# Four-token loads for nine units, shifts in a weight conversion, and low halves on GpSimd: a gated linear attention with FFN on one core

## The chip, the cores and the metric

The kernel runs on one core of a Trainium2 chip. The metric is the time of one execution on the device in microseconds (us). A core has five engines with instruction queues of their own: TensorE (PE, matmuls), VectorE (DVE), ScalarE (ACT), GpSimd (POOL) and SyncE (SP, which here issues the DMAs). Data lies in SBUF, matmul results in PSUM.

## The reference

Attention runs over batch, head and time with a decaying state of 48 x 48; its output, put together by token, goes through a feed-forward network (FFN).

```python
B, H, S, D = 4, 8, 768, 48
for t in range(S):
    state = alpha[:, :, t, :, None] * state + np.einsum('bhd,bhe->bhde', k[:, :, t], v[:, :, t])
    y[:, :, t] = np.einsum('bhd,bhde->bhe', q[:, :, t], state)
x = y.transpose(0, 2, 1, 3).reshape(B * S, H * D)     # 3072 x 384
h = x @ w_in                                          # w_in 384 x 2048, float64
g = np.maximum(0.01 * h, h)
out = (g @ w_out).astype(np.float32)                  # w_out 2048 x 384, float64
```

## The kernel before, in words

**Units and blocks.** A unit is 128 tokens of one batch entry, all 8 heads: 6 time blocks by 4 entries, 24 units. Three units make a block of 384 tokens for the FFN, 8 blocks in all. The hidden width of 2048 is cut into 16 pieces of 128, counted by f; (i, f) is the FFN item of block i and piece f.

**A unit** (`attention`) is written as steps that a generator yields. `scans` turns alpha so that the head dimension lies on partitions and time along the row, and makes the running products `pc` (L309) and the reverse sums `rc` (L315). `scaled_q` and `scaled_k` turn q and k and multiply them by `pc` and `rc`. `scores` and `mask_scores` make and mask the 128 x 128 scores (PE L351, ACT L361, POOL L362), `outputs` the result and its split into xh and xl (L419, L420), `next_state` the new state (`us` at L430 or L432, scaled on POOL at L367). Tiles of loads have two buffers each for alpha, q and k, three for v; the load of unit u+2 is asked for as soon as unit u's tile has been turned.

For the first nine units (`AHEAD`) a load puts a token's row in a partition: 128 x 8 runs of 48 numbers (192 bytes). `transposed` turns such a tile by four PE transposes of 128 x 128 (L272). For the later units four tokens follow one another in a run, and DVE turns them (L284, STREAM_TRANSPOSE).

**Weights.** They come as float64 words in the tile `raw` (four buffers), and `converting` makes of each piece f a high and a low part (`w`, 128 x 768 each): ACT scales the upper words in place (L238); DVE makes the float32 `bits` (L240, L243); ACT rounds these to the matmul format, `hi` (L246); DVE takes the exponent, `pw` (L250), subtracts `hi` from the value (L252), scales the lower words by `pw` (L254) and adds both into `lo` (L257). All DVE operations here are 128 x 768.

**An FFN item.** `ffn_in` runs nine matmuls of 384 columns into `ph` (L487): for each of three row groups high x xh, high x xl, low x xh. ACT makes `t` = 0.01 ph (L490), DVE the maximum (L493), ACT the high half `gh` (L495), DVE the low half `gl` = t - gh (L499). `ffn_out` runs nine matmuls of 384 columns (L512) three items later (`LAG`); `gl` has four buffers, `t` two.

**The order.** A scheduler sets the order on each engine from the program's order and its own estimates; `issue_after` holds an instruction behind another in it. First come nine units (the front); the weights of pieces 0 and 1 are loaded and converted among the last of them, and item (0,0) and (1,0) too. Then the items of blocks 0 and 1 alternate, (0, f), (1, f), while piece by piece is loaded and converted; `put` writes these DVE and ACT steps one behind another in a fixed line. From block 2 on attention of units 9 to 23 is cut in slices between items; its first eight steps are held behind the `gl` of the item before (`behind("gl", ...)`).

Of the kernel before, what the change touches and what calls it, by code (L numbers as in the profile page):

```python
# [22 lines left out]
def gated_linear_attn_ffn(ctx, tc, q, k, v, alpha, w_in, w_out, out):  # L23
# [31 lines left out]
    T4 = 4  # L55
# [1 line left out]
    PITCH = RUN + GAP  # L57
    AHEAD = 3 * UPB
    LAG = 3
    SOON, EARLY = 2, 2  # L60
    LEAD = 8
    SL = 8 * UPB

# [52 lines left out]
    def load(u, i):  # L116
        if u >= NU:
            return
        if u >= AHEAD and later is not None:
            later.append((load, u, i))  # L120
            return
        tb, b = units[u]
        ts = slice(tb * C, (tb + 1) * C)
        t, src = loaded(u, i), (alpha, q, k)[i]
        if u < AHEAD:
            n = H if u or i else H // 2
            for h in range(0, H, n):
                nc.sync.dma_start(
                    by_token(t)[:, h:h + n, 0:D], src[b, h:h + n, ts, :].rearrange("h t d -> t h d")
                )  # L130
            return

        for a in range(4):
            off = 32 * (a % 2)
            nc.sync.dma_start(
                t[32 * a:32 * (a + 1), :].rearrange("j (p r) -> j p r", p=NP)[:, :, 0:RUN - off],
                src[b, a // 2::2, ts, :].rearrange("p (j t) d -> j p (t d)", t=T4)[:, :, off:],
            )
# [12 lines left out]

    nc.vector.memset(seed, 0.0)
    nc.vector.memset(ones, 1.0)
    zeros = cst.tile([P, 4 * C], F32R, name="zeros")
    nc.gpsimd.memset(zeros.bitcast(F32), 0.0)

    idle = ps_h.tile([P, 512], F32, name="ph")

# [2 lines left out]
        for _ in range(n):  # L161
            nc.tensor.matmul(idle[:, 0:C], seed[:, 0, :], seed[:, 1, :], start=True, stop=True)

    def keep_warm_wide(n):

        for _ in range(2):
            nc.tensor.matmul(idle[:, 0:n], zeros[:, 0:P], zeros[:, 0:n], start=True, stop=True)

    keep_warm(6)
    for i in (0, 1, 2):  # L170
        for t in loads_sb[i]:
            nc.vector.memset(by_token(t)[:, :, D:], 1.0)
    for n in range(max(NL)):
        for i in range(3):
            if n < NL[i]:
# [7 lines left out]
    )  # L183
    for i in (0, 1, 2):
        for t in loads_sb[i]:
            nc.gpsimd.memset(t[:, H * HB:], 1.0)


    runs = [(0, D, 0, 1, D), (D, GAP, NG * D, NG, 1), (HB, D, NP * D, 1, D), (BR, GAP, (NP + NG) * D, NG, 1)]
# [29 lines left out]
    def converting(f, ordered=False):  # L219

        if f >= NF:
            return
        raw = jobs.pop(f)
        w_sb[f] = cst.tile([P, 2, 2 * DM], F32R, name=f"w{f}")
        hi, lo = w_sb[f][:, HIGH, :], w_sb[f][:, LOW, :]
        if not f64:
            val = raw[:, :, 0:P].bitcast(F32)
            hi, lo = (t.rearrange("p (g f) -> p g f", f=P) for t in (hi, lo))
            nc.scalar.copy(hi, val)
            made["w", f] = nc.vector.tensor_tensor(lo, val, hi.bitcast(F32), ALU.subtract)  # L230
            return
        words = raw.rearrange("p g (f w) -> p (g f) w", w=2)
        top, low = words[:, :, 1], words[:, :, 0]
        bits = cvp.tile([P, 2 * DM], I32, name="bits", bufs=NBITS)
        val = bits.bitcast(F32)

        with nullcontext() if lines["ACT"] else behind("hi", f - 1):
            put(ordered, "ACT", lambda: nc.scalar.mul(top.bitcast(F32), top.bitcast(F32), 2.0 ** -112))  # L238
        yield
        put(ordered, "DVE", lambda: nc.vector.tensor_scalar(  # L240
            bits, top, 3, 0x7FFFFFF8, ALU.logical_shift_left, ALU.bitwise_and))
        yield
        put(ordered, "DVE", lambda: nc.vector.scalar_tensor_tensor(  # L243
            bits, top, -0x80000000, bits, ALU.bitwise_and, ALU.bitwise_or))
        yield
        made["hi", f] = put(ordered, "ACT", lambda: nc.scalar.copy(hi, val))  # L246
        yield
        pw = cvp.tile([P, 2 * DM], I32, name="pw", bufs=NPW)
        rest = pw.bitcast(F32)
        put(ordered, "DVE", lambda: nc.vector.tensor_scalar(pw, bits, -0x800000, None, ALU.bitwise_and))  # L250
        yield
        put(ordered, "DVE", lambda: nc.vector.tensor_tensor(val, val, hi.bitcast(F32), ALU.subtract))  # L252
        yield
        put(ordered, "DVE", lambda: nc.vector.scalar_tensor_tensor(  # L254
            rest, low.bitcast(U32), 2.0 ** -52, rest, ALU.mult, ALU.mult))
        yield
        made["w", f] = put(ordered, "DVE", lambda: nc.vector.tensor_tensor(lo, rest, val, ALU.add))  # L257

    def convert(f):
        for _ in converting(f):  # L260
# [5 lines left out]
    def transposed(u, i, name, **kw):  # L266

        src = loaded(u, i)
        if u < AHEAD:
            ps = banks4()  # L270
            for p in range(NP):
                last = nc.tensor.transpose(  # L272
                    ps[:, p, :], by_token(src)[:, 2 * p:2 * p + 2, :].rearrange("t h d -> t (h d)"), ident
                )
                if u == 0 and p % 2:
                    with tc.issue_after(last.ins):
                        if i == 2:
                            keep_warm_wide(4 * C if p == 1 else 2 * C)
                        else:
                            keep_warm(2)  # L280
            return ps
        t = atp.tile([P, NP, C], F32, name=name, **kw)
        src = src.rearrange("r (p n) -> r p n", p=NP)[:, :, 0:RUN]
        nc.vector.transpose(  # L284
            t.rearrange("r p (j t) -> r p t j", t=T4),
            src.rearrange("r p (t d) -> r p t d", t=T4)[:, :, :, 0:32],
        )
        return t
# [189 lines left out]
    def ffn_in(i, f, steps=None):  # L478

        ordered = steps is not None  # L480
        first, second = steps or ((), ())
        xh, xl = xs[i]
        ph = ps_h.tile([P, 512], F32, name="ph")[:, 0:TB]
        n = 0
        for g in range(NG):
            for wn, xt in ((HIGH, xh), (HIGH, xl), (LOW, xh)):
                nc.tensor.matmul(ph, w_in_of(f, wn, g), xt[:, g, :], start=n == 0, stop=n == 3 * NG - 1)  # L487
                n += 1
        t = ffp.tile([P, TB], F32, name="t")
        put(ordered, "ACT", lambda: nc.scalar.mul(t, ph, 0.01))  # L490
        for step in first:
            next(step, None)
        put(ordered, "DVE", lambda: nc.vector.tensor_tensor(t, ph, t, ALU.max))  # L493
        gh = ffp.tile([P, TB], F32R, name="gh", bufs=LAG + 1)
        put(ordered, "ACT", lambda: nc.scalar.copy(gh, t))  # L495
        for step in second:
            next(step, None)
        gl = ffp.tile([P, TB], F32R, name="gl", bufs=LAG + 1)
        made["gl", i, f] = put(ordered, "DVE", lambda: nc.vector.tensor_tensor(gl, t, gh.bitcast(F32), ALU.subtract))  # L499
        return gh, gl  # L500

    pos = {}
# [53 lines left out]
                gs[len(gs)] = ffn_in(i, f)  # L556
    kinds[:] = "a"

    with behind("x", AHEAD - 1):
        for _ in converting(EARLY, True):  # L560
            pass

    due, emitted, held = 0.0, 0, 0
    new, coming = None, converting(EARLY + 1, True)
    next(coming)
    for n in range(len(items) + LAG):
        slices = 0
        if n < len(items):
            i, f, slices, _ = items[n]
            if f == 0:  # L570
                if i == 2:
                    st, held = attention(AHEAD, NU), 8
                while i not in ready:
                    next(st)
                emitted, due = 0, 0.0
            if loaded_f < NF:
                load_weights(loaded_f)
                loaded_f += 1
                if loaded_f == NF:
                    asked, later = later, None  # L580
                    with behind("raw", NF - 1):
                        for fn, *args in asked:
                            fn(*args)
            if n < len(STARTS):
                pass
            elif i == 0:
                old, new, coming = new or iter(()), coming, converting(f + SOON + 1, True)
                gs[n] = ffn_in(i, f, ((), (coming, new, old, new)))
            elif i == 1:
                gs[n] = ffn_in(i, f, ((new, new), (new,)))  # L590
                next(new, None)
            else:
                gs[n] = ffn_in(i, f)
        for half in range(2):
            due += slices / 2
            while emitted < due:

                with behind("gl", *items[n - 1][:2]) if held else nullcontext():
                    next(st, None)
                held = max(held - 1, 0)  # L600
                emitted += 1
            if half == 0 and n >= LAG:
                i, f, _, tag = items[n - LAG]
                ffn_out(i, f, gs.pop(n - LAG), tag)
# [131 lines left out]
```

## Time and profile before

| what | value |
|---|---|
| median of 3 runs | 540.11 us (539.74 to 540.44) |
| the profiled execution | 538.77 us |
| its span in the profile | 537.1 us |
| PE busy | 518.8 us (97%) |
| DVE busy | 375.0 us (70%) |
| ACT busy | 234.0 us (44%) |
| POOL busy | 49.1 us (9%) |
| DMA, mean over the span | 87 GB/s |

The profile shows one execution, whose span begins with its first and ends with its last instruction. PE is busy nearly all the time; what it does not fill lies mostly in the first 80 us, so a reader should go by stretches of the span, not by shares of the whole. A row of instructions gives line, engine, operation, the tile written and the tiles read, the busy time and the mean of one in ns, and the idle time of that engine ahead of it with what ended it. The chain is followed back from the last instruction: each piece has its start, its length and what it was.

### The profile page before, as it was taken

The page shows a single profiled execution, that of the slowest core. Times are in us where ns is not written, and L with a number is a line of the kernel's source. Part 1 is how long each engine was busy: PE and PEld are TensorE (multiplying, and loading weights), DVE is VectorE, ACT ScalarE, POOL GpSimd, SP SyncE. Part 2 cuts the span into 40 slices and gives each one's busy share as a digit, 9 for nine tenths or more (in the row PEclk, how much of TensorE's full clock was granted, in tenths as well). Part 3 has the DMA queues.
Part 4 walks back from the last instruction along what each step waited for, and adds up shares of the span by engine and source line. Part 5 has one row for each costly group of instructions (what it writes and reads, how often), then busy time and mean ns, then how long its engine had stood idle before and what let it go on. Part 6 is the DMA issues. An engine that isn't in the chain of part 4 may idle for free.

```text
span 537.1 us, 10383 instructions
## 1 busy us (share of the span) xinstructions
PE 518.8 (97%) x3934; PEld 492.6 (92%) x3934; DVE 375.0 (70%) x703; ACT 234.0 (44%) x514; POOL 49.1 (9%) x116
## 2 busy tenths in 40 slices
PE   8879899999999999999999999999999999999995
PEld 7668789999999899999999999999999999999995
DVE  6778999999988897875675685775777534332331
ACT  2665755555533453435334443344343354233331
POOL 3333510000000011010000001000000000000000
PEclk9999899999999999999999999999999999999998
DMA  9999854454823643533323422523201010001001
GB/s 149 163 179 183 198 140 119 117 131 136 183 53 87 190 117 78 107 81 98 70 67 70 108 69 64 98 50 92 71 0 38 11 35 1 22 1 45 1 1 49
DMA packets 92985, 46.67 MB, mean 87 GB/s; under 512 B 57856, under 2 KB 90112, under 8 KB 92928
## 3 DMA queue, kind: packets, MB, share of 16 engines
q1 hardware_dynamic: 92928, 45.93, 39.0%
q8 instruction: 33, 0.54, 0.4%
q14 instruction: 24, 0.20, 0.1%
HBM read 38.83 MB, written 4.72 MB: 81 GB/s over the span
## 4 chain that ended last, share of the span: by engine, by line
PE 86%; DVE 4%; DMA 3%; issue 2%; ACT 1%; SPq 1%; POOL 1%; ACTq 0%; DVEq 0%; POOLq 0%
PE ph L487 36%; PE b L512 32%; PE a L390 5%; PE a L351 4%; PE a L512 4%; DMA small<-in_alpha_dram 2%; DMA raw<-in_moe_w_in_dram 1%; PE a L374 1%; PE b L272 1%; PE a L411 1%; PE b L390 1%; DVE pc L309 1%; PE b L411 1%; POOL sm L362 1%; DVE rc L315 0%
## 5 line engine op out<-in xcount | busy, mean ns | idle before, releaser
L487 PE MATMUL ph<-large,w 128*128 128x384 f32 x1152 | 227.4, 340 | 2.8 <-DVE t L493 2.8
L487 PEld LDWEIGHTS ph<-large,w 128*128 128x128 f32 x1152 | 201.9, 189 | 5.5 <-DVE t L493 3.9
L512 PE MATMUL b<-w,gh 128*128 128x384 f32 x672 | 170.0, 340 | 0.0
L493 DVE TENSOR_TENSOR t<-ph,t 128x384 f32<-128x384 f32 x128 | 70.5, 551 | 88.7 <-ACT t L490 88.4
L512 PEld LDWEIGHTS b<-w,gh 128*128 128x128 f32 x672 | 119.7, 188 | 2.2 <-issue 0.5
L490 ACT ACTIVATE t<-ph 128x384 f32<-128x384 f32 x128 | 62.6, 489 | 130.1 <-PE ph L487 122.8
L495 ACT CAST gh<-t 128x384 fp32r<-128x384 f32 x128 | 65.7, 514 | 112.8 <-DVE t L493 102.6
L512 PE MATMUL b<-w,gl 128*128 128x384 f32 x336 | 107.4, 336 | 0.0
L499 DVE TENSOR_TENSOR gl<-t,gh 128x384 fp32r<-128x384 f32 x128 | 70.8, 553 | 34.4 <-ACT gh L495 33.2
L512 PEld LDWEIGHTS b<-w,gl 128*128 128x128 f32 x336 | 62.5, 188 | 0.1
L362 POOL TENSOR_SCALAR_AFFINE_SELECT sm<-sm 128x512 f32<-128x512 f32 x33 | 22.8, 705 | 113.3 <-ACT sm L361 113.3
L351 PE MATMUL a<-qs,ks 48*128 48x128 f32 x312 | 30.9, 287 | 0.1
L351 PEld LDWEIGHTS a<-qs,ks 48*128 48x128 f32 x312 | 25.9, 189 | 5.4 <-issue 4.4
L284 DVE STREAM_TRANSPOSE ks<-small 128x512 f32<-128x512 f32 x15 | 16.6, 1121 | 12.3 <-PE a L374 12.3
L390 PE MATMUL a<-sm,small 128*48 128x128 f32 (+1 forms) x312 | 23.2, 282 | 0.1
L319 POOL COPY pe<-pc 128x4 f32<-128x4 f32 x24 | 4.8, 202 | 188.6 <-DVE pc L309 188.6
L309 DVE TENSOR_TENSOR_SCAN pc<-e,small 128x128 f32<-128x128 f32 x60 | 20.1, 398 | 0.5 <-ACT pc L327 0.5
L367 POOL TENSOR_TENSOR small<-us,pe 112x192 f32<-112x192 f32 x20 | 11.9, 594 | 90.2 <-DVE us L432 87.5
L390 PEld LDWEIGHTS a<-sm,small 128*48 128x48 f32 (+1 forms) x312 | 17.1, 132 | 3.2 <-issue 3.0
L361 ACT COPY sm<-a 128x512 f32<-128x512 f32 x24 | 14.0, 585 | 13.8 <-PE b L351 11.1
L512 PE MATMUL a<-w,gh 128*128 128x384 f32 x96 | 20.0, 336 | 0.0
L315 DVE TENSOR_TENSOR_SCAN rc<-e,small 128x511 f32<-128x511 f32 x15 | 19.0, 1270 | 0.2
(86 smaller groups left out, 525.4 us busy)
## 6 DMA issues: line engine op xcount, KB each, us to landing
raw<-in_moe_w_out_dram SPq DMA_DIRECT2D x16, 384.0 KB, 3.9
small<-in_v_dram SPq DMA_DIRECT2D x24, 192.0 KB, 4.0
raw<-in_moe_w_in_dram SPq DMA_DIRECT2D x32, 144.0 KB, 3.9
out_dram<-t SPq DMA_DIRECT2D x24, 192.0 KB, 1.9
small<-in_alpha_dram SPq DMA_DIRECT2D x32, 96.0 KB, 2.3
small<-in_q_dram SPq DMA_DIRECT2D x30, 96.0 KB, 2.2
small<-in_k_dram SPq DMA_DIRECT2D x30, 96.0 KB, 2.2
small<-in_alpha_dram SPq DMA_DIRECT2D x30, 80.0 KB, 2.3
```

What stands on the lines that cost most here:

```text
L284: nc.vector.transpose(t.rearrange("r p (j t) -> r p t j", t=T4), src.rearrange("r p (t d) -> r p t d", t=T4)[:, :, :, 0:32],)
L309: nc.vector.tensor_tensor_scan(pc[:, p, :], aT[:, p, :], ones.broadcast_to([P, C]), 1.0, ALU.mult, ALU.mult)
L315: nc.vector.tensor_tensor_scan(flat[2][:, NP * C - 2::-1], flat[0][:, NP * C - 1:0:-1], flat[1][:, NP * C - 2::-1], last, ALU.mult, ALU.add)
L351: nc.tensor.matmul(ss[s][:, p, :], ks[lo:lo + D, p, :], qs[lo:lo + D, p, :], start=True, stop=True)
L362: nc.gpsimd.affine_select(out=sm[s], in_=sm[s], compare_op=ALU.is_ge, fill=0.0, base=0, pattern=[[0, NP], [1, C]], channel_multiplier=-1)
L390: nc.tensor.matmul(y[s][HB * c:HB * c + lhsT.shape[-1], p % 2, :], lhsT, rhs, skip_group_check=True, **kw)
L487: nc.tensor.matmul(ph, w_in_of(f, wn, g), xt[:, g, :], start=n == 0, stop=n == 3 * NG - 1)
L490: put(ordered, "ACT", lambda: nc.scalar.mul(t, ph, 0.01))
L493: put(ordered, "DVE", lambda: nc.vector.tensor_tensor(t, ph, t, ALU.max))
L495: put(ordered, "ACT", lambda: nc.scalar.copy(gh, t))
L499: made["gl", i, f] = put(ordered, "DVE", lambda: nc.vector.tensor_tensor(gl, t, gh.bitcast(F32), ALU.subtract))
L512: nc.tensor.matmul(po[j], gt[:, js], w_out_of(f, wn), start=f == 0 and n == 0, stop=f == NF - 1 and n == 2)
```

## The change

Five things are changed.

1. **Loads of the first nine units.** Each load of alpha, q and k is two DMAs, one for the even and one for the odd heads. A partition holds four tokens that follow one another of one head: 128 runs of 192 numbers (768 bytes) in each DMA. Unit 0's alpha had been loaded in two halves of heads before.
2. **Their turn.** Instead of four transposes, eight matmuls against the identity: for each of the four tokens in a run and each half, 128 x 64 stationary, 128 columns moving, written to every fourth column of 64 partitions of the PSUM bank. The fills of gaps ahead of the first load are adapted (128 x 2 x 16 instead of 128 x 8 x 16 on DVE, 128 x 416 instead of 128 x 320 on POOL). The tile `zeros` with its fill and the wide matmuls that keep PE active in unit 0 are gone; every turn of unit 0 has two times two small ones.
3. **Conversion.** `bits` gets a set low bit; the subtraction L252 becomes two shifts of the upper word in place (top << 23 >> 23, one input), and the last two operations are scalar_tensor_tensor: low * 2^-32 + top, then that * 2^-20 * pw. The low part no longer waits for ACT's `hi`.
4. **Order of the conversion.** Three steps of piece 2 stand ahead of the loop. In item (0, f) the conversion of piece f+1 is finished, in item (1, f) the first two DVE steps of f+2 are done.
5. **Low halves.** `gl` of blocks 0 and 1, 32 instructions, runs on POOL.

```diff
         if u < AHEAD:
-            n = H if u or i else H // 2
-            for h in range(0, H, n):
+            for s in (0, 1):
                 nc.sync.dma_start(
-                    by_token(t)[:, h:h + n, 0:D], src[b, h:h + n, ts, :].rearrange("h t d -> t h d")
+                    t[:, s * PITCH:s * PITCH + RUN],
+                    src[b, s::2, ts, :].rearrange("p (j t) d -> p j (t d)", t=T4),
                 )
...
-            bits, top, 3, 0x7FFFFFF8, ALU.logical_shift_left, ALU.bitwise_and))
+            bits, top, 3, 4, ALU.logical_shift_left, ALU.bitwise_or))
...
-        put(ordered, "DVE", lambda: nc.vector.tensor_tensor(val, val, hi.bitcast(F32), ALU.subtract))
+        put(ordered, "DVE", lambda: nc.vector.tensor_scalar(
+            top, top, 23, 23, ALU.logical_shift_left, ALU.arith_shift_right))
         yield
+        rest = top.bitcast(F32)
         put(ordered, "DVE", lambda: nc.vector.scalar_tensor_tensor(
-            rest, low.bitcast(U32), 2.0 ** -52, rest, ALU.mult, ALU.mult))
+            rest, low.bitcast(U32), 2.0 ** -32, top, ALU.mult, ALU.add))
         yield
-        made["w", f] = put(ordered, "DVE", lambda: nc.vector.tensor_tensor(lo, rest, val, ALU.add))
+        made["w", f] = put(ordered, "DVE", lambda: nc.vector.scalar_tensor_tensor(
+            lo, rest, 2.0 ** -20, pw.bitcast(F32), ALU.mult, ALU.mult))
...
-            ps = banks4()
-            for p in range(NP):
-                last = nc.tensor.transpose(
-                    ps[:, p, :], by_token(src)[:, 2 * p:2 * p + 2, :].rearrange("t h d -> t (h d)"), ident
-                )
+            ps = bank()
+            for n in range(T4):
+                for s in (0, 1):
+                    at = s * PITCH + n * D
+                    last = nc.tensor.matmul(
+                        ps[HB * s:HB * (s + 1), n::T4], src[:, at:at + HB], ident, start=True, stop=True, skip_group_check=True
+                    )
...
-        made["gl", i, f] = put(ordered, "DVE", lambda: nc.vector.tensor_tensor(gl, t, gh.bitcast(F32), ALU.subtract))
+        if i < 2:
+            made["gl", i, f] = nc.gpsimd.tensor_tensor(gl, t, gh.bitcast(F32), ALU.subtract)
+        else:
+            made["gl", i, f] = nc.vector.tensor_tensor(gl, t, gh.bitcast(F32), ALU.subtract)
...
+    new, coming = converting(EARLY, True), converting(EARLY + 1, True)
     with behind("x", AHEAD - 1):
-        for _ in converting(EARLY, True):
-            pass
+        for _ in range(3):
+            next(new)
...
             elif i == 0:
-                old, new, coming = new or iter(()), coming, converting(f + SOON + 1, True)
-                gs[n] = ffn_in(i, f, ((), (coming, new, old, new)))
+                gs[n] = ffn_in(i, f, ((new, new), (coming, new, new, new)))
             elif i == 1:
-                gs[n] = ffn_in(i, f, ((new, new), (new,)))
-                next(new, None)
+                gs[n] = ffn_in(i, f, ((), (coming, coming)))
+                new, coming = coming, converting(f + EARLY + 1, True)
```

The order on SP where the first weights are asked for, before. `raw` is the weight tile, its four rows from L202 are the w_in part of piece 0; the row of alpha is unit 6's, that of v unit 5's.

```order
L206 DMA raw<-in_moe_w_out_dram 128x384 [waits DMAHW6_49]
L128 DMA small<-in_q_dram 128x8x48 [waits DMAHW7_49,PE_49]
L128 DMA small<-in_k_dram 128x8x48 [waits DMAHW0_49,PE_49]
L128 DMA small<-in_alpha_dram 128x8x48 [waits DMAHW1_49,PE_49]
L147 DMA small<-in_v_dram 128x8x48 [waits DMAHW2_49,PE_49]
L202 DMA raw<-in_moe_w_in_dram 48x3x128 [waits DMAHW3_49]
L202 DMA raw<-in_moe_w_in_dram 48x3x128 [waits DMAHW4_49]
```

And in the changed kernel, whose lines are numbered anew (loads at L127, w_in at L198):

```order
L127 DMA small<-in_k_dram 128x1x192 [waits DMAHW1_49,PE_49]
L147 DMA small<-in_v_dram 128x8x48 [waits DMAHW2_49,PE_49]
L198 DMA raw<-in_moe_w_in_dram 48x3x128 [waits DMAHW3_49]
L198 DMA raw<-in_moe_w_in_dram 48x3x128 [waits DMAHW4_49]
L198 DMA raw<-in_moe_w_in_dram 16x3x128 [waits DMAHW5_49]
L198 DMA raw<-in_moe_w_in_dram 16x3x128 [waits DMAHW6_49]
L127 DMA small<-in_alpha_dram 128x1x192 [waits DMAHW7_49,PE_49]
L127 DMA small<-in_alpha_dram 128x1x192 [waits DMAHW0_49,PE_49]
```

Unit 6's alpha has moved behind the four pieces of w_in; unit 5's values (L147) still stand ahead of them.

The order on DVE in the conversions of pieces 12 and 13, before. `t` is the maximum of an item, `w_1761` and `w_1824` are weight pieces.

```order
L493 TENSOR_TENSOR t<-ph,t 128x384 [waits Activation_49]
L252 TENSOR_TENSOR bits<-bits,w_1761 128x768 [waits DVE_49,Activation_49]
L499 TENSOR_TENSOR gl<-t,gh 128x384 [waits PE_49,Activation_49]
L254 SCALAR_TENSOR_TENSOR pw<-raw,pw 128x768
L493 TENSOR_TENSOR t<-ph,t 128x384 [waits Activation_49]
L240 TENSOR_SCALAR bits<-raw 128x768 [waits DMAHW6_49,DMAHW2_49,DMAHW7_49,DMAHW1_49,DMAHW0_49]
L257 TENSOR_TENSOR w_1761<-pw,bits 128x768 [waits DVE_49]
L243 SCALAR_TENSOR_TENSOR bits<-raw,bits 128x768 [waits DVE_49]
L499 TENSOR_TENSOR gl<-t,gh 128x384 [waits PE_49,Activation_49]
L250 TENSOR_SCALAR pw<-bits 128x768 [waits DVE_49]
```

And in the changed kernel, behind the maximum of item (0, 11); `e`, `qs` and `pc` are unit 9's, L281 DVE's transpose, L306 the scan, `w_1825` weight piece 12:

```order
L490 TENSOR_TENSOR t<-ph,t 128x384 [waits Activation_49]
L247 TENSOR_SCALAR raw<-raw 128x768
L281 STREAM_TRANSPOSE e<-small 128x4x4x32 [waits DMAHW3_49,DMAHW4_49,DMAHW2_49,DMAHW1_49]
L251 SCALAR_TENSOR_TENSOR raw<-raw 128x768 [waits DVE_49]
L306 SCALAR_TENSOR_TENSOR pc<-e,small 128x128 [waits DVE_49]
L306 SCALAR_TENSOR_TENSOR pc<-e,small 128x128 x3
L281 STREAM_TRANSPOSE qs<-small 128x4x4x32 [waits DMAHW6_49,DMAHW7_49,DMAHW5_49,DMAHW0_49]
L254 SCALAR_TENSOR_TENSOR w_1825<-raw,pw 128x768 [waits DVE_49]
L490 TENSOR_TENSOR t<-ph,t 128x384 [waits Activation_49]
L236 TENSOR_SCALAR bits<-raw 128x768
```

The low halves (L499) have left DVE, the subtraction has become the shift at L247, and unit 9's transposes and scans, which stood behind the last conversion, stand inside that of piece 12; the rest of them follows in that of piece 13.

More of the change, by code (lines that the diff above doesn't have):

```diff
@@ L59, in gated_linear_attn_ffn @@
     LAG = 3
-    SOON, EARLY = 2, 2
+    EARLY = 2
     LEAD = 8
@@ L153, in gated_linear_attn_ffn @@
     nc.vector.memset(ones, 1.0)
-    zeros = cst.tile([P, 4 * C], F32R, name="zeros")
-    nc.gpsimd.memset(zeros.bitcast(F32), 0.0)
     idle = ps_h.tile([P, 512], F32, name="ph")
@@ L162, in keep_warm, with tails @@
             nc.tensor.matmul(idle[:, 0:C], seed[:, 0, :], seed[:, 1, :], start=True, stop=True)
-    def keep_warm_wide(n):
-        for _ in range(2):
-            nc.tensor.matmul(idle[:, 0:n], zeros[:, 0:P], zeros[:, 0:n], start=True, stop=True)
     keep_warm(6)
+    def tails(t):
+        return t[:, 0:2 * PITCH].rearrange("r (s n) -> r s n", s=2)[:, :, RUN:]
     for i in (0, 1, 2):
         for t in loads_sb[i]:
-            nc.vector.memset(by_token(t)[:, :, D:], 1.0)
+            nc.vector.memset(tails(t), 1.0)
     for n in range(max(NL)):
@@ L185, in gated_linear_attn_ffn @@
         for t in loads_sb[i]:
-            nc.gpsimd.memset(t[:, H * HB:], 1.0)
+            nc.gpsimd.memset(t[:, 2 * PITCH:], 1.0)
     runs = [(0, D, 0, 1, D), (D, GAP, NG * D, NG, 1), (HB, D, NP * D, 1, D), (BR, GAP, (NP + NG) * D, NG, 1)]
@@ L248, in converting @@
         pw = cvp.tile([P, 2 * DM], I32, name="pw", bufs=NPW)
-        rest = pw.bitcast(F32)
         put(ordered, "DVE", lambda: nc.vector.tensor_scalar(pw, bits, -0x800000, None, ALU.bitwise_and))
         yield
-        put(ordered, "DVE", lambda: nc.vector.tensor_tensor(val, val, hi.bitcast(F32), ALU.subtract))
+        put(ordered, "DVE", lambda: nc.vector.tensor_scalar(
+            top, top, 23, 23, ALU.logical_shift_left, ALU.arith_shift_right))
         yield
+        rest = top.bitcast(F32)
         put(ordered, "DVE", lambda: nc.vector.scalar_tensor_tensor(
-            rest, low.bitcast(U32), 2.0 ** -52, rest, ALU.mult, ALU.mult))
+            rest, low.bitcast(U32), 2.0 ** -32, top, ALU.mult, ALU.add))
         yield
-        made["w", f] = put(ordered, "DVE", lambda: nc.vector.tensor_tensor(lo, rest, val, ALU.add))
+        made["w", f] = put(ordered, "DVE", lambda: nc.vector.scalar_tensor_tensor(
+            lo, rest, 2.0 ** -20, pw.bitcast(F32), ALU.mult, ALU.mult))
     def convert(f):
@@ L269, in transposed @@
         if u < AHEAD:
-            ps = banks4()
-            for p in range(NP):
-                last = nc.tensor.transpose(
-                    ps[:, p, :], by_token(src)[:, 2 * p:2 * p + 2, :].rearrange("t h d -> t (h d)"), ident
-                )
-                if u == 0 and p % 2:
-                    with tc.issue_after(last.ins):
[L277 to L281, printed above, removed]
+            ps = bank()
[5 more added lines that the diff above has]
+                    )
+                if u == 0 and n % 2:
+                    with tc.issue_after(last.ins):
+                        keep_warm(2)
+            return ps.rearrange("r (p t) -> r p t", p=NP)
         t = atp.tile([P, NP, C], F32, name=name, **kw)
@@ L557, in gated_linear_attn_ffn @@
     kinds[:] = "a"
+    new, coming = converting(EARLY, True), converting(EARLY + 1, True)
     with behind("x", AHEAD - 1):
-        for _ in converting(EARLY, True):
-            pass
+        for _ in range(3):
+            next(new)
     due, emitted, held = 0.0, 0, 0
-    new, coming = None, converting(EARLY + 1, True)
-    next(coming)
     for n in range(len(items) + LAG):
```

## The prediction

> **What bounds the kernel now.** I read the page first, then PE's busy time by stretches, then the chain of waits, then what PE and ACT waited for.
>
> ```profile
> span 537.1 us, 10383 instructions
> ...
> PE 518.8 (97%) x3934; PEld 492.6 (92%) x3934; DVE 375.0 (70%) x703; ACT 234.0 (44%) x514; POOL 49.1 (9%) x116
> ...
> PE 86%; DVE 4%; DMA 3%; issue 2%; ACT 1%; SPq 1%; POOL 1%; ACTq 0%; DVEq 0%; POOLq 0%
> ```
>
> PE is busy for 97% and carries 86% of the chain. So only two things can move the end: PE's idle time, 18.3 us in all, and the time in which PE runs at less than its full clock. The stretches (columns: PE, PEld, DVE, ACT, POOL busy, granted clock, DMA share, GB/s) say where both lie:
>
> ```profile
> 30.00:40.00 10.00, 7.30 (x98) 5.84 (x100) 6.91 (x17) 6.56 (x17) 3.29 (x7) 0.96 0.95 160
> 40.00:50.00 10.00, 9.78 (x130) 8.57 (x127) 8.29 (x21) 5.81 (x15) 2.48 (x7) 0.87 1.08 183
> 50.00:60.00 10.00, 8.37 (x131) 6.92 (x129) 9.96 (x19) 6.21 (x16) 6.15 (x8) 0.98 1.06 198
> 60.00:70.00 10.00, 10.00 (x93) 8.42 (x93) 9.06 (x16) 7.14 (x17) 3.00 (x3) 0.85 0.77 215
> 80.00:160.00 80.00, 80.00 (x461) 79.99 (x461) 79.37 (x128) 42.24 (x75) 0.00 (x0) 1.00 0.50 124
> ```
>
> The front (the first nine units, up to about 80 us) has gaps and a low clock. From 80 to 160 us, the weight conversions, PE has no gap, and DVE hardly one. The chain, in pieces:
>
> ```profile
> 9.78 4.62 DMA small<-in_alpha_dram
> ...
> 33.21 2.68 DMA raw<-in_moe_w_in_dram
> ...
> 60.05 3.15 PE ph L487 x9
> ...
> 79.81 1.56 PE ph L487 x9
> ```
>
> A load of alpha and the first weight load stand in it, and the first FFN item takes 3.15 us where a later one takes 1.56: half the clock. What PE and ACT waited for in the front:
>
> ```profile
> L272 PE MATMUL b<-small 128*128 128x128 f32 x68 | 10.8, 281 | 3.9 <-ACT us L430 2.0 <-DMA small<-in_alpha_dram 1.7 <-DVE rc L315 0.2
> ```
>
> ```profile
> ACT raw L238 <- DMA raw<-in_moe_w_in_dram: 2.6, 1, 2.6
> ```
>
> ```profile
> PE b L390 <- DVE rc L315: 1.5, 1, 1.5
> PE ph L487 <- DVE t L493: 0.9, 1, 0.9
> ```
>
> So the turns waited 1.7 us for alpha, and 2.0 us for ACT, which itself stood 2.6 us in its first conversion step for weights that had not landed. DVE held PE for 1.5 and 0.9 us later.
>
> **The loads (1).** Each of the 27 loads of 1,024 runs becomes two of 128 runs.
>
> ```profile
> small<-in_alpha_dram SPq DMA_DIRECT2D x8, 192.0 KB, 5.6
> ...
> small<-in_alpha_dram SPq DMA_DIRECT2D x2, 96.0 KB, 2.5
> ```
>
> A whole load landed after 5.6 us; the two half loads of unit 0, in the old short runs, after 2.5. No row shows the new halves at this place; 2.5 us, and one issue later for the second, is taken. SP's own queue ahead of the first weights:
>
> ```profile
> 26.73 3.17 SPq L128 DMA_DIRECT2D small<-in_alpha_dram  x1
> 30.00 0.90 SPq L147 DMA_DIRECT2D small<-in_v_dram  x1
> 30.95 2.84 SPq L202 DMA_DIRECT2D raw<-in_moe_w_in_dram  x4
> ```
>
> An issue of 1,024 runs that waits for nothing takes 0.90 us (L147), one of 144 or 48 runs (L202) 2.84 / 4 = 0.71. Two of the new ones may thus cost SP up to 0.5 more than one old one, 27 x 0.5 = 13.5 us spread over 65; SP's slack covers it, and without that cover it would eat this part's gain. Most of the gain is slack too: unit after unit is started by a ring through POOL and ACT, not by alpha. The ceiling is the 1.7 us, the floor 0; taken **-0.6**.
>
> The first weights gain more surely. Their issue at 30.95 stood behind that of unit 6's alpha, which held SP for 3.17 us; in the new order it stands ahead of that. Of PE's 2.0 us, between 0 and all, taken **-1.6**: the values of unit 5 stay ahead of it, with their own waits. The low clock follows the pauses: 7.30 busy of 10, then 0.87; 8.37 of 10, then 0.85 and the 3.15 us item. A clock of 0.87 and 0.85 over 10 us each is 1.3 + 1.5 = 2.8 us of PE time; a shorter first pause may spare the first part. Taken **-1.0** of 0 to 2.8.
>
> **The turns (2).** Eight matmuls a load instead of four transposes. Nearest rows, PE at full clock:
>
> ```profile
> 26.86 0.51 PE a L390 x8
> ...
> 29.00 0.44 PE b L272 x4
> ```
>
> L390 also writes alternate halves of the partitions, as the new ones do, so 0.07 us more a load, 27 x 0.07 = 1.9. If the two halves don't run side by side, eight take 0.88, and 27 x 0.44 = 11.9, most of it in the front's gaps; if the short stationary saves, nothing. Half of 1.9 falls on the path: **+0.9**. The output is written with a stride of four, which no row shows; it would hit the same term. The smaller fills of POOL and DVE lie ahead of the first load's landing: 0.
>
> **Conversion and low halves (3, 4).** In 80 to 160 us:
>
> ```profile
> L499 DVE TENSOR_TENSOR gl<-t,gh 128x384 fp32r<-128x384 f32 x27 | 14.9, 553 | 0.6 <-ACT gh L495 0.6
> ...
> L252 DVE TENSOR_TENSOR bits<-bits,w 128x768 f32<-128x768 f32 x13 | 12.3, 949 | 0.0
> ...
> L250 DVE TENSOR_SCALAR pw<-bits 128x768 int32<-128x768 int32 x12 | 6.7, 554 | 0.0
> ```
>
> DVE's records overlap at their ends, so starts count:
>
> ```profile
> 65.14 0.95 DVE L254 SCALAR_TENSOR_TENSOR pw<-raw,pw 128x768 f32<-128x768 uint32 x1
> 66.01 0.99 DVE L499 TENSOR_TENSOR gl<-t,gh 128x384 fp32r<-128x384 f32 x1
> 66.92 1.38 DVE L257 TENSOR_TENSOR w<-pw,bits 128x768 fp32r<-128x768 f32 x1
> ...
> 69.35 0.56 DVE L499 TENSOR_TENSOR gl<-t,gh 128x384 fp32r<-128x384 f32 x1 [0.58 <-ACT gh L495]
> 69.82 0.42 DVE L420 TENSOR_TENSOR large<-b,large 112x256 fp32r<-112x256 f32 x1
> ```
>
> A 768-wide operation occupies 0.87 us (65.14 to 66.01), a 384-wide one 0.47 (69.35 to 69.82). The subtraction L252 becomes a one-input shift like L250, whose 0.55 us record is that of a 384-wide one: -0.40 a block; the last two keep their width. The two low halves leave: -0.94. PE's period per weight block is 36 matmuls, 36 x 80/461 = 6.25 us; DVE's falls from 6.20 (6.25 less 0.6/13 idle) to 4.86. PE fills 80.00 of 80: the gain **there is 0**. It counts only where DVE held PE: 1.5 + 0.9 = 2.4 us before 80 us. Two conversions (0.80) and three low halves (1.41) of 2.2 us lie ahead of those waits; PE takes some back: **-1.6**, bounds 0 and -2.4.
>
> What do the low halves cost on POOL?
>
> ```profile
> 43.87 1.22 POOL L362 TENSOR_SCALAR_AFFINE_SELECT sm<-sm 128x512 f32<-128x512 f32 x2
> ...
> 50.04 0.51 POOL L367 TENSOR_TENSOR small<-us,pe 112x192 f32<-112x192 f32 x1 [2.13 <-DVE us L432]
> ...
> 65.18 2.31 POOL L362 TENSOR_SCALAR_AFFINE_SELECT sm<-sm 128x512 f32<-128x512 f32 x2 [1.39 <-ACT sm L361]
> ```
>
> ```profile
> L319 POOL COPY pe<-pc 128x4 f32<-128x4 f32 x24 | 4.8, 202 | 188.6 <-DVE pc L309 188.6
> ```
>
> Two-input POOL work 192 wide takes 0.51 alone, a tiny copy 0.20; 384 wide is 0.20 + 2 x 0.31 = 0.82 (at most 1.02, twice the row). POOL does nothing else there, and a low half is used three items later, some 9 us. But the pair at 65.18 took 2.31 instead of 1.22, and beside it gl took 0.99 instead of 0.55 and L257 1.38 instead of 0.95: the engines hold each other up, DVE by 0.44 and 0.43 for 0.61 of POOL, 0.18 less than its duration. Two low halves then cost DVE 2 x (0.82 - 0.18) = 1.28, and 4.86 + 1.28 = 6.14 us, just under 6.25. I take **0**; the bounds are none and 2 x 1.02.
>
> The Trainium skill speaks against it: "SBUF — State Buffer", section "SBUF: two separate sides", has the port pair that VectorE and GpSimd share as an exclusive lock, held for the whole instruction, so that the other one stands. By that DVE would lose 2 x 0.82 and have a period of 6.50 us (the third rival). The rows at 66 us agree that each stands for the other, though DVE for 0.18 us less than POOL's duration.
>
> **Unit 9 (5).** With the last low half of item 31 on POOL, unit 9's transposes and scans are no longer held on DVE; the order puts them into conversions 12 and 13, behind their alpha and q loads, which SP now issues ahead of the last weights.
>
> ```profile
> 165.09 1.10 DVE L284 STREAM_TRANSPOSE e<-small 128x512 f32<-128x512 f32 x1
> 166.03 1.09 DVE L284 STREAM_TRANSPOSE qs<-small 128x512 f32<-128x512 f32 x1
> 166.95 1.33 DVE L309 TENSOR_TENSOR_SCAN pc<-e,small 128x128 f32<-128x128 f32 x4
> ...
> 169.44 1.30 DVE L315 TENSOR_TENSOR_SCAN rc<-e,small 128x511 f32<-128x511 f32 x1
> ```
>
> ```profile
> PE ph L487 <- DVE t L493: 1.8, 2, 1.0
> ```
>
> With the reciprocal and the product it is some 5.2 us of DVE. Two periods spare 2 x 0.1 (with POOL in the way) to 2 x 1.4, so 2.4 to 5.0 us are late; w12's low part can be some 1.2 late (PE wants it three groups and two matmuls after the item, 3 x 1.56 + 0.35 = 5.03 us; it is ready after ACT's step, some 0.55, and DVE's 0.47 + 0.47 + 0.87 + 0.87 with one hold-up of 0.64, 3.87), so PE would stand 1.2 to 3.8. Waiting behind the transpose are w12's and w13's parts, and behind those PE. In return the hole of 1.8 us behind the transition (the row above, 160 to 182 us) closes. Taken **+0.6**, bounds -1.8 and +3.8.
>
> **Sum.** -0.6 - 1.6 - 1.0 + 0.9 - 1.6 + 0.6 = -3.3 us. The profiled execution took 538.77 us (1.67 around the span); that makes 535.5. The median of the runs is 540.11, 1.34 above it: **536.8**.
>
> **Rivals.** *Larger:* the whole 1.7, 2.0 and 2.8 us go: 1.1 + 0.4 + 1.8 = 3.3 more, 533.5. For it speaks that these waits follow one another in the chain; against, that PE's order in the front also waits for POOL and ACT. *Hidden:* units follow the ring, so the first three terms give half (+1.6), and unit 9 costs 1.8 (+1.2): 539.6. For it: alpha's wait is only 1.7 of 80 us. *Other side, the shared port:* if DVE stands for POOL's whole 0.82 us, the period is 6.50, 0.25 over PE's, and in 13 periods (81 us) 3.3 us: 540.1. At 1.02 it is 6.90, 0.65 x 13 = 8.5: 545.3. It decides from 0.70 us of hold-up per low half (4.86 + 1.39 = 6.25), and undoes the gain from 0.82. For it: the doubled POOL rows; against: the 0.18. That the change does not do what it says: the order of the changed kernel has the low halves on POOL and the loads in pairs, so it gets no chance.
>
> **How the numbers follow.** The summed case has 0.45 (its own range 534.5 to 539); larger 0.15; hidden 0.17; the port 0.23, half of it at 541 and more. The measurement can tell about 0.2%, 1.1 us, from no change: 539.0 to 541.2. Faster: 0.43 + 0.15 + 0.05 + 0.03 = 0.66. Same: 0.02 + 0.10 + 0.07 = 0.19. Slower: the rest, 0.02 + 0.13 = 0.15. The range 532.5 to 543.0 leaves out about a tenth at each end.
>
> **What would show it.** Right: alpha loads of two halves landing under 3 us and no wait for alpha at 14 us; ACT's wait for raw under 1 us; eight turns in 0.5 us; PE still 80 of 80 in the conversions, DVE near 6.1 busy per 6.25, low halves on POOL of 0.8 to 1.3 us. Wrong: PE waiting for t or for w in that stretch (the port), eight turns near 0.9, PE standing over 2 us for w12 some 20 us before the conversions end, or ACT's wait for raw as long as before.

## The result, and the profile after

The changed kernel takes 576.02 us (575.5 to 576.55), the kernel before beside it 539.92: a ratio of 1.067, 95% interval 1.065 to 1.069. It is 36 us slower where 3 us less were forecast. Its profiled execution has a span of 574.3 us, 37.2 more than before. The page, with the rows that answer to those of before:

```profile
span 574.3 us, 11034 instructions
...
PE 545.8 (95%) x4262; PEld 511.3 (89%) x4262; DVE 376.8 (66%) x671; ACT 235.1 (41%) x514; POOL 96.6 (17%) x147
...
PE 74%; DVE 13%; DMA 7%; issue 3%; SPq 1%; ACT 1%; POOL 0%; DVEq 0%; ACTq 0%
```

PE's share of the chain fell from 86% to 74%; DVE went from 4% to 13%, DMA from 3% to 7%. PE also has 27 us more of recorded work and 328 more instructions. The stretches of the same profile (columns as before):

```profile
30.00:40.00 10.00, 7.89 (x106) 7.15 (x102) 5.17 (x12) 3.76 (x10) 2.17 (x6) 0.83 0.46 123
40.00:50.00 10.00, 7.36 (x109) 6.15 (x106) 3.46 (x7) 2.74 (x7) 1.71 (x5) 1.00 0.46 125
50.00:60.00 10.00, 4.26 (x54) 3.22 (x55) 4.81 (x11) 4.36 (x11) 2.05 (x5) 0.87 0.43 107
60.00:70.00 10.00, 10.00 (x156) 9.06 (x154) 5.65 (x13) 4.11 (x11) 2.05 (x5) 0.79 0.49 135
80.00:160.00 80.00, 76.58 (x507) 69.77 (x507) 72.26 (x96) 40.91 (x78) 37.12 (x28) 0.98 0.49 128
```

Between 30 and 60 us PE, DVE and ACT all stand idle for part of the time, and from 30 up to 70 us the DMA engines are only 0.43 to 0.49 busy where they were 0.77 to 1.08. The maximum `t` of an item (DVE, one for each item of blocks 0 and 1, in the order (0,0), (1,0), (0,1) ...) is a good milestone. From the timelines:

| milestone | before, us | after, us | lost so far | lost since |
|---|---|---|---|---|
| 5th `t`, item (0,2) | 81.34 | 107.37 | 26.0 | 26.0 in the front |
| 23rd `t`, item (0,11) | 137.86 | 168.96 | 31.1 | 5.1 in nine weight blocks |
| 25th `t`, item (0,12) | 144.14 | 180.60 | 36.5 | 5.4 in one weight block |
| 32nd `t`, item (1,15) | 163.42 | 201.69 | 38.3 | 1.8 in the last blocks |
| end of the span | 537.1 | 574.3 | 37.2 | -1.1 |

So there are three losses: a large one in the front, a steady one in the conversions, and one where unit 9's steps stand. The chain of the changed kernel in the front:

```profile
2.24 4.57 DMA small<-in_alpha_dram
...
18.71 1.02 PE b L272 x16
...
27.85 5.43 DMA small<-in_k_dram
...
38.74 6.42 DMA small<-in_alpha_dram
...
49.96 3.30 DMA raw<-in_moe_w_in_dram
...
76.49 7.14 DMA small<-in_k_dram
```

Half a load takes 4.6 to 7.1 us to land, where a whole one took 5.6, and a turn is 16 recorded matmuls in 1.02 us where four transposes took 0.44. ACT's first conversion step waited for the late weights, and everything on ACT behind it:

```profile
ACT raw L234 <- DMA raw<-in_moe_w_in_dram: 10.4, 1, 10.4
```

One weight block in the conversions, DVE and POOL, after:

```profile
124.69 0.54 DVE L490 TENSOR_TENSOR t<-ph,t 128x384 f32<-128x384 f32 x1
125.16 0.54 DVE L236 TENSOR_SCALAR bits<-raw 128x768 int32<-128x768 int32 x1
125.73 0.96 DVE L239 SCALAR_TENSOR_TENSOR bits<-raw,bits 128x768 int32<-128x768 int32 x1
126.73 1.26 DVE L245 TENSOR_SCALAR pw<-bits 128x768 int32<-128x768 int32 x1
127.91 0.54 DVE L490 TENSOR_TENSOR t<-ph,t 128x384 f32<-128x384 f32 x1
128.38 0.54 DVE L247 TENSOR_SCALAR raw<-raw 128x768 int32<-128x768 int32 x1
128.96 0.96 DVE L251 SCALAR_TENSOR_TENSOR raw<-raw 128x768 f32<-128x768 uint32 x1
129.95 1.65 DVE L254 SCALAR_TENSOR_TENSOR w<-raw,pw 128x768 fp32r<-128x768 f32 x1
131.53 0.54 DVE L490 TENSOR_TENSOR t<-ph,t 128x384 f32<-128x384 f32 x1
```

```profile
125.86 1.71 POOL L497 TENSOR_TENSOR gl<-t,gh 128x384 fp32r<-128x384 f32 x1 [1.91 <-ACT gh L492]
129.08 1.71 POOL L497 TENSOR_TENSOR gl<-t,gh 128x384 fp32r<-128x384 f32 x1 [1.51 <-ACT gh L492]
```

From 124.69 to 131.53 a block takes 6.84 us, and DVE has no gap of its own in it: it is the bound. A low half on POOL starts while DVE's L239 or L251 runs, and ends some 0.87 us after that has ended (129.92 and 130.79). The DVE operation behind it is stretched by 0.71: L245 from 0.55 to 1.26, L254 from 0.95 to 1.65. Where DVE stands idle beside it, a low half takes 1.01:

```profile
199.07 1.01 POOL L497 TENSOR_TENSOR gl<-t,gh 128x384 fp32r<-128x384 f32 x1 [1.91 <-ACT gh L492]
```

So POOL waits for DVE, and DVE then for most of POOL's work.

### The profile page after: what moved, and what is told of

Its sections match the earlier page's. It is cut to its first block, busy times and chain, and to the rows that moved or that the text cites. A ratio compares the mean times of both kernels' runs of the same rounds, so it can differ in the third digit from the quotient of the medians.

```text
span 574.3 us, 11034 instructions
## 1 busy us (share of the span) xinstructions
PE 545.8 (95%) x4262; PEld 511.3 (89%) x4262; DVE 376.8 (66%) x671; ACT 235.1 (41%) x514; POOL 96.6 (17%) x147
## 4 chain that ended last, share of the span: by engine, by line
PE 74%; DVE 13%; DMA 7%; issue 3%; SPq 1%; ACT 1%; POOL 0%; DVEq 0%; ACTq 0%
PE ph L484 28%; PE b L512 27%; PE a L387 5%; PE a L348 4%; PE b L272 3%; DMA small<-in_alpha_dram 2%; DMA small<-in_k_dram 2%; DVE pw L245 2%; DVE t L490 2%; DVE bits L239 2%; DVE raw L251 2%; PE a L272 2%; DVE w L254 1%; DMA raw<-in_moe_w_in_dram 1%; PE a L371 1%
## 5 line engine op out<-in xcount | busy, mean ns | idle before, releaser
L499 DVE TENSOR_TENSOR gl<-t,gh 128x384 fp32r<-128x384 f32 x96 | 52.8, 550 | 33.3 <-ACT gh L492 32.1
L497 POOL TENSOR_TENSOR gl<-t,gh 128x384 fp32r<-128x384 f32 x32 | 50.3, 1572 | 56.6 <-ACT gh L492 56.6
L272 PE MATMUL b<-small 128*64 128x128 f32 x272 | 25.9, 309 | 2.9 <-DMA small<-in_alpha_dram 2.4
L417 DVE TENSOR_TENSOR large<-a,large 112x256 fp32r<-112x256 f32 x39 | 15.2, 416 | 18.1 <-ACT large L416 18.1
L281 DVE STREAM_TRANSPOSE ks<-small 128x512 f32<-128x512 f32 x15 | 16.8, 1123 | 12.9 <-PE a L371 12.9
L272 PE MATMUL a<-small 128*64 128x128 f32 x160 | 17.0, 306 | 8.3 <-DMA small<-in_k_dram 7.6
L254 DVE SCALAR_TENSOR_TENSOR w<-raw,pw 128x768 fp32r<-128x768 f32 x16 | 24.5, 1530 | 0.5
L272 PEld LDWEIGHTS b<-small 128*64 128x64 f32 x272 | 20.2, 155 | 4.8 <-issue 2.2
L387 PE MATMUL a<-sm,small 128*64 128x128 f32 (+1 forms) x312 | 24.1, 282 | 0.0
```

Of the source, the lines that this page charges most:

```text
L254: made["w", f] = put(ordered, "DVE", lambda: nc.vector.scalar_tensor_tensor(lo, rest, 2.0 ** -20, pw.bitcast(F32), ALU.mult, ALU.mult))
L272: last = nc.tensor.matmul(ps[HB * s:HB * (s + 1), n::T4], src[:, at:at + HB], ident, start=True, stop=True, skip_group_check=True)
L387: nc.tensor.matmul(y[s][HB * c:HB * c + lhsT.shape[-1], p % 2, :], lhsT, rhs, skip_group_check=True, **kw)
L497: made["gl", i, f] = nc.gpsimd.tensor_tensor(gl, t, gh.bitcast(F32), ALU.subtract)
L499: made["gl", i, f] = nc.vector.tensor_tensor(gl, t, gh.bitcast(F32), ALU.subtract)
```

## The experiments

Theory: the loads cost the front, the port that POOL and DVE share costs the conversions, and unit 9 costs one block. Rivals: the conversion's new order or POOL's work delays the front; late weights, not the port, slow the conversions.

**Old loads in the changed kernel** (`load`, `transposed`, the fills and the active-keeping matmuls as before; everything else of the change stays).

> The changed kernel with the loads and turns of the first nine units as they were before (the matmuls that keep PE active and the zeros tile with them); conversion, order and POOL's low halves stay. Theory (of the 36 us, 26 are lost in the front through the new loads, 6 to 8 to the port shared by POOL and DVE in the conversions, 4 to unit 9's work in conversions 12 and 13): 550 us (547 to 553), the period of a weight block stays near 6.84 us. Rival (the front is late through POOL's low halves and the new conversion order, not the loads): above 565 us.

Measured: 550.82 us, ratio 1.022 (1.020 to 1.023). The loads and turns cost 25 us; the rival is out. Its fifth maximum comes at 81.12 us, as before (81.34), and a weight block still takes 6.85.

**The loads alone in the kernel before.**

> The kernel before with nothing but the new loads and turns of the first nine units. Theory (the loads alone cost 26 us): 566 us (562 to 570). Rival (the loss of the front needs the new conversion or order as well): 540 to 550 us.

Measured: 569.36 us, ratio 1.057 (1.055 to 1.058), 30 us. They need nothing else of the change.

**The same bytes in another order.**

```diff
-                    src[b, s::2, ts, :].rearrange("p (j t) d -> p j (t d)", t=T4),
+                    src[b, s::2, ts, :].rearrange("p (j t) d -> j p (t d)", t=T4),
...
-                        ..., src[:, at:at + HB], ident, start=True, ...
+                        ..., src[:, at:at + HB], ident.rearrange("r (j p) -> r p j", p=NP), start=True, ...
```

> The changed kernel with one difference: in the loads of the first nine units partition 4j + p, not 32p + j, holds group j of four tokens of head pair p, so that the outermost count of each DMA is 32 and not 4; the identity's columns are read in the matching order. Runs, bytes and number of DMAs are the same. Theory (a DMA is spread over DMA engines by its outermost count, so the changed kernel's loads went through about four of sixteen): landings fall from over 4.5 to 2 to 3 us, the mean busy share of the DMA engines in the first 9 us rises from 0.22 to above 0.6, the first maximum t of item (0,0) comes at 60 to 66 us instead of 92, 550 us (547 to 553). Rival 1 (fewer, larger runs or the doubled number of issues are slow in themselves): within 3 us of 576. Rival 2 (the eight turning matmuls cost the front): above 565.

Measured: 574.72 us, ratio 1.066 (1.065 to 1.068). The time says rival 1, the profile says otherwise. The first 9 us of the changed kernel, then of this one, and this one's landings:

```profile
0.00:9.00 9.00, 6.42 (x26) 4.85 (x26) 0.74 (x8) 1.28 (x1) 3.40 (x14) 1.00 0.19 61
```

```profile
0.00:9.00 9.00, 7.46 (x44) 5.98 (x46) 1.88 (x12) 1.28 (x1) 3.41 (x14) 1.00 0.44 112
```

```profile
small<-in_alpha_dram SPq DMA_DIRECT2D x4, 96.0 KB, 2.5
small<-in_q_dram SPq DMA_DIRECT2D x4, 96.0 KB, 2.6
small<-in_k_dram SPq DMA_DIRECT2D x4, 96.0 KB, 2.5
```

The loads land in 2.5 us, as said. The share over these 9 us rose from 0.19 to 0.44, not to above 0.6; but in the first 2 us of them nothing moves. From 4 to 9 us, the changed kernel and then this run:

```profile
4.00:9.00 5.00, 3.95 (x17) 2.38 (x15) 0.00 (x0) 0.00 (x0) 0.04 (x1) 1.00 0.27 90
```

```profile
4.00:9.00 5.00, 5.00 (x35) 3.51 (x35) 1.15 (x4) 0.00 (x0) 0.05 (x1) 1.00 0.59 152
```

0.27 of sixteen engines is 4.3, and 0.59 is 9.4. But PE has taken the loads' place. A turn in this run's chain:

```profile
27.28 1.84 PE b L272 x16
```

1.84 us instead of 1.02: the moving identity (the operand that streams past the stationary one) is read in steps of four. My remedy had a price of its own that hid its success.

**The permuted identity written once.** The loads are those of the run before. A tile `turn` holds the permuted identity, and the turns read it in unit steps.

```diff
+    turn = cst.tile([P, C], F32, name="turn")
+    nc.gpsimd.tensor_copy(turn.rearrange("r (p j) -> r p j", p=NP), ident.rearrange("r (j p) -> r p j", p=NP))
```

> The run with partition 4j + p again, but the permuted identity is written once to a tile of its own (by POOL, ahead of the first turn), so that the turns read it in unit steps. Theory (the spread load lands in 2.5 us; in the run before PE paid for reading the identity in steps of four, 0.12 us a matmul instead of 0.055 to 0.064): a turn of 16 recorded matmuls takes 0.9 to 1.0 us instead of 1.95, against 0.44 for the old four transposes; 27 x 0.5 = 13.5 us more PE work than before in the front, of which its gaps hide some 8: 555 us (551 to 560). Rival (the steps of the identity are not what made it slow): within 4 us of 574.7.

Measured: 556.03 us, ratio 1.030 (1.025 to 1.034). The turn in its chain:

```profile
26.43 0.87 PE b L274 x16
```

In the changed kernel's chain, too, a turn takes 1.02 or 0.87 us, so the turns are the same in both. Of the front's loss 20 us (576.0 to 556.0) are the order of the loads' dimensions alone.

**Cheap turns, without and with the spread loads.** Both leave out the heads' right arrangement, as the expectations say.

```diff
-                for s in (0, 1):
-                    at = s * PITCH + n * D
-                    last = nc.tensor.matmul(
-                        ps[HB * s:HB * (s + 1), n::T4], src[:, at:at + HB], ident, start=True, stop=True, skip_group_check=True
-                    )
+                last = nc.tensor.transpose(ps[:, n::T4], src[:, n * D:n * D + P], ident)
```

> The changed kernel with its own loads, but the eight matmuls of a turn are replaced by four transposes of 128 contiguous columns, written to every fourth column; this leaves out the right arrangement of heads (the numbers that come out are others), and keeps loads, waits and all other work. Theory (loads through about four DMA engines set the front by themselves: 27 x 2 x 96 KB at some 92 GB/s is 56 us, besides v and weights): 570 to 576 us, PE waits for the loads longer. Rival (the two passes of the turns are what costs): 552 to 560 us.

> Both taken away: loads with partition 4j + p and four transposes a turn (with the same part left out, the right arrangement of heads). Theory (spreading and turn cost make up the whole loss of the front): 550 us (546 to 552), as with the old loads, unit cadence 5.6 us or less. Rival (something else in the new front, the order on SP or the conversion, loses too): above 556.

Measured: 576.84 us (ratio 1.068, 1.063 to 1.074) and 553.25 us (1.025, 1.021 to 1.030). With the loads as they were, cheap turns gain nothing: PE only waits longer. With spread loads they gain 2.8 us. The second came out above its range and 2.4 above the old loads' 550.8, though the intervals of the two ratios overlap. PE waits 5.2 us for ACT's `us` there, behind the first weights, where it waited 4.5 with the old loads. Twice the issues on SP are not why: `w_in` is asked for at 30.30 us there and at 30.98 with the old loads, and ACT's step on it starts at 35.53 and 36.60. What makes the 2.4 stays open.

**All low halves on DVE again.**

> The changed kernel with all low halves on DVE again (at their place in the fixed line of steps); loads, turns and conversion stay new. Theory (POOL's low halves hold DVE up by 0.71 us each and let unit 9's work into the conversions): period 6.25 us instead of 6.84, no wait of PE for w near 174 us, 13 x 0.59 + 4 less: 564.5 us (562 to 567). Rival (the conversions are slow because the late loads of weights push into them): 573 to 577 us, period unchanged.

Measured: 565.37 us, ratio 1.048 (1.046 to 1.050); 10.65 us back (10.3 by the ratios). PE has no gap again:

```profile
110.00:160.00 50.00, 50.00 (x289) 50.00 (x288) 49.17 (x81) 27.70 (x48) 0.00 (x0) 1.00 0.45 127
```

289 matmuls in 50 us are 36 in 6.23, and L245 and L254 take 0.55 and 0.96 us again. The weights come as late as in the changed kernel (ACT stands 10.7 us for them, there 10.4), so lateness isn't what stretched the blocks.

**Unit 9 held on DVE.** The low halves stay on POOL, the hold of the first eight steps goes to the maximum.

```diff
-        put(ordered, "DVE", lambda: nc.vector.tensor_tensor(t, ph, t, ALU.max))
+        made["t", i, f] = put(ordered, "DVE", lambda: nc.vector.tensor_tensor(t, ph, t, ALU.max))
...
-                with behind("gl", *items[n - 1][:2]) if held else nullcontext():
+                with behind("t", *items[n - 1][:2]) if held else nullcontext():
```

> The changed kernel with unit 9's first eight steps held behind DVE's maximum t of item (1,15) instead of behind POOL's low half of it; all else stays. Theory (unit 9's work in conversions 12 and 13 costs 4.8 us there and gives 1 back behind the transition): 572 us (570.5 to 573.5), no wait of PE for w. Rival (it is neutral): 575 to 577.

Measured: 572.71 us, ratio 1.060 (1.056 to 1.065) against 1.067: 3.8 us by the ratios, which just don't overlap, and 3.3 by the times. This wait of the changed kernel, from 160 to 200 us, is gone:

```profile
PE ph L484 <- DVE w L254: 3.3, 1, 3.3
```

**Half of the low halves on POOL** (block 0's; block 1's on DVE in the line).

> The changed kernel, but only block 0's low halves run on POOL; block 1's are on DVE at their place in the fixed line (the held steps of unit 9 are then held on DVE again). Theory (a low half on POOL holds DVE up by 0.71 us, on DVE it takes 0.47; DVE's steps of a weight block make 5.43 without low halves, so 5.43 + 0.71 + 0.47 = 6.61 us against PE's 6.25): about halfway between the two in the stretch, period 6.5 to 6.6, and nothing lost to unit 9: 569 us (567 to 570.5). Rival (DVE has room for one on POOL, period 6.25): 565 us, as with all on DVE.

Measured: 567.15 us, ratio 1.051 (1.048 to 1.053). The stretch:

```profile
110.00:160.00 50.00, 50.00 (x281) 48.46 (x280) 49.21 (x72) 27.21 (x47) 12.53 (x8) 1.00 0.47 127
```

The maxima of block 0 come every 6.49 us. One low half on POOL is already too many: the period shows it, where the time alone would not (this run's interval overlaps that of the run with all on DVE, 1.046 to 1.050). The sum of 6.61 was 0.12 too high: the low half on DVE stands between L239 and L245, which then don't follow each other directly (see below on low halves).

**What is left without loads and POOL:** old loads, low halves on DVE, the new conversion and its order.

> Old loads and turns, all low halves on DVE; what is left of the change is the conversion with shifts and its order (parts 3 and 4). Theory (the three losses add: 550.8 less 10.65, the difference that taking the low halves back made on the changed kernel): 540 us (538.5 to 541.5), no gain over the kernel before, since PE fills the conversions there and ACT's wait for the first weights (4.5 us with old loads and the new order, 2.0 before) takes what the front gains. Rival (the conversion gains by itself where DVE bounds): 535 to 537.

Measured: 537.38 us, ratio 0.994 (0.992 to 0.996), above the rival's range by 0.4 and below the theory's. My theory missed: the losses don't simply add, since PE waits 2.0 us for ACT's `us` here, as before, and not the 4.5 of the first run. Parts 3 and 4 are a small gain, some 2.6 us (2 to 4 by the interval).

**ACT's first conversion step later.**

```diff
-        with nullcontext() if lines["ACT"] else behind("hi", f - 1):
+        with nullcontext() if lines["ACT"] else behind(*(("hi", f - 1) if f else ("xh", 5))):
```

> The run before it, with ACT's first conversion step (the scaling of piece 0) held behind unit 5's copy xh instead of ahead of unit 3's state. Theory (ACT stands still there for weights that have not landed, and unit 3's state and with it PE wait behind it): PE's wait for ACT's us goes from 4.5 to 0, ACT waits less than 0.5 us for raw, 536.5 us (534 to 538.5). Rival (the wait is hidden by the ring through POOL and ACT anyway, or the front then waits for the next load): within 1 us of the run before it.

> The kernel before with that one edit. Theory: 2.0 us of PE's wait go, and some of the 0.87 clock behind it: 537 us (535.5 to 538.5). Rival (hidden): 539 to 540.

Measured: 535.70 us (0.992, 0.990 to 0.995) and 536.04 us (0.994, 0.991 to 0.996). PE's waits between 25 and 60 us, without and with the edit (the runs with parts 3 and 4):

```profile
PE b L275 <- ACT us L433: 2.0, 1, 2.0
```

```profile
PE b L275 <- DMA small<-in_alpha_dram: 1.9, 2, 1.2
```

The wait for ACT is gone in full, and one for alpha has come up. On top of parts 3 and 4 the edit gains 1.7 us, with overlapping intervals; in the kernel before it gains 4.0 us, twice the wait. But in the two profiled executions, 2.6 us apart, PE does not stand idle for less: span less busy time is 534.5 - 516.4 = 18.1 us with the edit, where it was 18.3. PE's busy time fell instead, from 518.8 to 516.4 us for the same 3934 records. The granted clock answers to that: its mean over the span was 0.996 to 0.999 in the six runs with the edit and 0.987 to 0.994 in the twelve of the kernel before. The stretch from 40 to 50 us had 0.87 and that from 60 to 70 us 0.85; with the edit the first

```profile
40.00:50.00 10.00, 8.59 (x120) 6.71 (x120) 8.37 (x19) 6.82 (x17) 3.75 (x8) 1.00 1.05 184
```

runs at 1.00, and the other too. Both runs beat both kernels; which of the two is better their intervals don't tell.

## Why the prediction was wrong, point by point

**The loads, -0.6.** This step failed, and took with it the two behind it: with their turns the loads cost 25 us, 20 of them by the order of dimensions. I took 2.5 us for a half load from a row of the old form, 128 tokens outermost, and set the floor at "no gain", with no reason that excluded a loss; the new halves took 4.6 to 7.1 us. Their outermost count is the four pairs of heads, and the DMA engines were 0.27 busy from 4 to 9 us, the share of some four of sixteen; with 32 outermost, and nothing else of the load changed, 0.59. The Trainium skill has the rule: "DMA: Bandwidth & Descriptors", section "Why a DMA increments its semaphore by 16 and not by 1", says that a DMA runs on the largest number of engines up to 16 that divides the slowest dimension of both its sides, here 4. The traces agree, by the shares above; no row here counts the engines of one DMA. The diff showed the order of dimensions, and I looked only at the size of the runs.

**ACT's stop, -1.6.** ACT's wait became 10.4 us instead of 2.6, and PE's behind it 2.4 instead of 2.0. `w_in` did move ahead of unit 6's alpha on SP, as the order showed, but with all queues ahead of it late it was asked for at 46.40 us instead of 30.95. Even where the loads land in time and SP has this order, in the run with spread loads and cheap turns, it is asked for at 30.30, only 0.65 sooner: the 3.17 us that alpha's issue had held SP do not come back as such. What took PE's wait away was ACT's own order.

**The clock, -1.0.** It fell to 0.83, 0.87 and 0.79 in three stretches instead of rising. That a pause brings the low clock isn't shown as a rule. In steps of 2 us PE is busy for 1.14 and 0.86 from 34 to 38 us in the kernel before, and the clock is then 0.78 and 0.50; with parts 3 and 4 alone it is busy for 1.36 and 0.59 in the same place, and the clock stays at 1.00 for the next 18 us. What decides it stays open.

**The turns, +0.9.** Mis-sized. "L390 x8" in 0.51 us is half of a unit's products: a float32 product is recorded as two matmuls, a transpose as one. Eight products are 16 records, 0.87 to 1.02 us, so 0.43 to 0.58 more than the old 0.44, at or above the upper bound of 0.44 that I had. With loads that land in time the path pays 2.8 us of it.

**Conversion, 0 in the stretch and -1.6 ahead of it.** Held where nothing else of the change is there: parts 3 and 4 gain 2.6 us, PE's period stays what it was (6.26 us a block, before 6.28), and PE's waits for DVE's `rc` fall from 1.7 to 0.5. In the changed kernel PE waits 2.2 us for `rc`, so the term didn't come there.

**Low halves, 0.** The rival of the other side came true; its bounds of 3.3 and 8.5 us hold the 7 (5.1 + 1.8) of the table. But its reason, the size of the hold-up, was not what I had most wrong. The hold-up is 0.71 us, between my 0.64 and the rival's 0.82; the low half itself takes 1.01 us, the upper bound, and not 0.82. The step that failed is DVE's own sum: the new line puts operations that need one another back to back, and such a start waits 0.10 to 0.13 us longer (L236 to L239 0.57, L247 to L251 0.58, L239 to L245 1.00, L251 to L254 0.99, where independent ones start 0.47 and 0.87 apart). 6.84 - 2 x 0.71 is 5.42, not 4.86. With 5.42 my hold-up would have given 6.70 and the rival's 7.06; the 6.84 lies between them. The rule of the Trainium skill that I weighed ("SBUF — State Buffer", section "SBUF: two separate sides", the exclusive lock) was right in its direction: the trace agrees that POOL waits for the end of DVE's operation and DVE then for POOL's, by 0.71 us and not the whole 1.01. That its 6.50 came nearer to 6.84 than my 6.14 is luck, since both had the same 4.86 in them.

**Unit 9, +0.6.** Mis-sized, at the edge of its bounds: 4.8 us in that block, 1.1 back, and 3.8 by the experiment. DVE was already the bound there, so nearly nothing of the 5.2 us could hide. (The rows of DVE's order that I showed of before are pieces 14 and 15, not 12 and 13; the line is the same in all of them.)

The range failed because the terms' bounds did. Had the port cost its 8.5 and unit 9 its 3.8, the sum would have been 536.8 + 8.5 + 3.2 = 548.5, and with the whole 11.9 of the turns 559.5. No term could hold 20 us from a load.

## What to carry to other kernels

Before costing a DMA by its bytes and runs, read which dimension is outermost on both sides: the same 96 KB took 2.5 us or over 4.5. Ask what work given to POOL costs DVE: here each low half took 0.47 us off DVE and put 0.71 on it, beside a one-input operation (L245) as beside a two-input one (L254). Sum both engines against the period, and add a tenth of a microsecond for each step that follows its own input. An engine that is idle most of the time can still matter by one early wait in its order: moving a single ACT step past a late transfer gained 4.0 us, more than the 2.6 of the new conversion. And look at where a gain appears: in the profiles that one came as a higher clock, not as less idle time.

## What the runs showed of the hardware that was not expected

- A float32 matmul against the identity of 128 x 64 by 128 columns is recorded twice, 0.054 to 0.064 us each (16 in 0.87 or 1.02); a transpose of 128 x 128 once, 0.11 (4 in 0.44).
- A moving operand read in steps of four took twice the time: 16 in 1.84 us instead of 0.87.
- A 384-wide subtraction of two inputs takes POOL 1.01 us beside an idle DVE, 1.71 with the wait for DVE.
- DVE starts an operation on the result of the one just before it 0.10 to 0.13 us later than an independent one.
- PE's granted clock was 0.50 for some microseconds behind some pauses of PE and 1.00 behind others as long.
